# Turning Q, K, P and the memory rows on four 128x32 column tiles instead of one 128x128 tile

## The chip, the core and the metric

The kernel runs on one core of one Trainium2 chip. The metric is the device time of one execution in microseconds; lower is better. Every time below comes from this kernel's runs or from the one execution that was profiled.

## What is computed

Two attention layers, written side by side into one output of 2048 tokens by 1280 columns, in bfloat16. The change touches only the second one, B, a recurrent memory transformer that goes through the tokens in segments of 32:

```python
mem = mem0                                             # 8 rows of 640
for s in range(n_seg):                                 # 64 segments
    h = concatenate([mem, x[:, 32 * s:32 * s + 32]])   # 40 tokens
    q, k, v = h @ Wq, h @ Wk, h @ Wv                   # 32 heads of 192
    p = softmax(mask(q @ k.T * scale))
    o = (p @ v) @ Wo                                   # 40 x 640
    mem = o[:, :8]                                     # into the next segment
    outs.append(o[:, 8:])
```

The first, A, is a sliding window attention over the same number of tokens. It stands ahead of B and is the same in both kernels.

## The kernel before

**Stages.** `part_a` runs first, for some 180 us. Then `part_b` runs 64 segments one after the other. A segment needs its memory rows from the segment before, so the segments are a chain. The 32 heads are handled in four groups `g` of eight; `segment` writes the order of all PE (TensorE) work by hand, and PE keeps that order. The orders on DVE (VectorE), ACT (ScalarE), POOL and SP are made by the framework's scheduler when the program is built, and are then fixed.

**Projections.** `project32` (L443) makes Q, K or V of 32 tokens for one group: for each of five slices of 128 input features, four matmuls, each with 128x32 stationary columns (the 32 tokens) and 384 moving weight columns, on four column tiles (`tile_position=(0, 32 * j)`), into four strips of 32 partitions of one accumulator `acc` (128x384, three buffers). Where a group is renewed (`RENEW`), the last 8 tokens of the next four segments are projected too, as a second set of 32 ("ahead"). `to_sb` casts an accumulator to `sb` (bf16).

**Turns.** `turn` (L456) transposes `sb`, strip by strip of 128 columns, by three matmuls against the identity, 128x128 stationary and 128 moving columns each, into a PSUM tile `pt`. `spread` copies `pt` into `QT`, `KT` or a waiting block `Lb`. `turn_late` does so for the ahead tokens. All copies out of PSUM go through `evacuate` (L423), which alternates between ACT and DVE.

**Attention.** `scores` (L515) takes `QT` and `KT`, on 128x64 and then on 64x64 tiles, into `Sps`. `softmax` runs on DVE (scale and mask L522, maximum `mx` L526, subtraction L527, sum `sm` L530, reciprocal L531) with the exponential on ACT (L528). `put_p` (L540) writes the weights `P` on DVE, two instructions, one for the 32 main tokens and one for the late ones. `turn_p` (L547) transposes both halves of `P` by two 128x128 transposes into a bf16 PSUM tile, copied to `PT`. `mix` (L564) multiplies `PT` with the values on 32x128 and 32x64 tiles, and `project_out` (L578) accumulates the output `Y` over the groups on 128x64 tiles.

**Seam of two segments.** ACT casts `Y` to `row` (L643); meanwhile PE finishes one ahead projection `ql`. `memory_rows` (L589) transposes the 8 memory rows of `row` into `pt` by six matmuls with 8 moving columns: four of 128x128, and between the second and the third of these two of 128x64. DVE copies the result into the next segment's input `HX` (L592). Then follows `turn_late` of `ql`, and the next segment's first projection, which reads `HX`.

**Weights.** Most weights stay in SBUF; 23 blocks of a segment's weights are streamed by SP through a ring of five slots (`t`), each load being issued when its slot comes free.

The order of a segment on PE around the turns, `tq`, `tk` being turns:

```python
tq[1] = project_qk(s, "q", 1)
tq[0]()
tk[0]()
tk[1] = project_qk(s, "k", 1)
put_p(s, 0, *softmax(scores(0)))
tq[1]()
tk[1]()
tq[2] = project_qk(s, "q", 2)
V[0] = values(s, 0)
soft = softmax(scores(1))
tq[2]()
PT[0] = turn_p()
put_p(s, 1, *soft)
tk[2] = project_qk(s, "k", 2)
mix(0, PT[0], V[0])
```

Of the kernel before, what the change touches and what calls it, by code (L numbers as in the profile page):

```python
# [7 lines left out]
FP32 = mybir.dt.float32  # L8
BF16 = mybir.dt.bfloat16
# [262 lines left out]
def part_b(ctx, tc, B_x, B_mem0, B_Wq, B_Wk, B_Wv, B_Wo, out, ident, n_seg, pre, nbuf, mid):  # L272
    nc = tc.nc
    Dm, H, Dh, M, SEG, L = 640, 32, 192, 8, 32, 40
# [92 lines left out]
    def pool(name, **kw):  # L367
        return ctx.enter_context(tc.tile_pool(name=name, reuse_waits="tile", **kw))
# [12 lines left out]
    ps_x = pool("b_ps_x", bufs=4, space=PSUM)  # L381
# [28 lines left out]
    P = cpool.tile([128, 2, 4, 32], BF16, name="P")  # L410
    OT = cpool.tile([128, 12 * L + PADW], BF16, name="OT")
    free = [cpool.tile([128, 12, M], BF16, name=f"Lb{i}") for i in range(BLOCKS)]
    late = {}
# [7 lines left out]
    def evacuate(dst, src):  # L421
        copies["n"] += 1
        (nc.scalar.copy if copies["n"] % 2 else nc.vector.tensor_copy)(dst, src)  # L423
# [24 lines left out]
    def to_sb(p):  # L448
        sb = qk_sb.tile([128, 384], BF16, tag="sb", name="sb")
        evacuate(sb[:], p[:])  # L450
        return sb

    def turn(sb):
        pt = ps_x.tile([128, 3, 4, 32], FP32, tag="x")
        for c in range(3):
            nc.tensor.matmul(pt[:, c], lhsT=sb[:, 128 * c:128 * c + 128], rhs=ident, start=True, stop=True)  # L456
        return pt

    def spread(dst, src):
# [5 lines left out]
    def turn_late(sb, m, g, s, start):  # L465

        pt = turn(sb)
        T = tokens(QT if m == "q" else KT)
        for t in range(start, next_start(m, g, start)):
            if t == s:  # L470
                dst = T[:, :, 32:L]
            else:
                late[m, g, t] = free.pop(0)
                dst = late[m, g, t][:]
            spread(dst, pt[:, :, :, M * (t % 4):M * (t % 4) + M])

    def project_qk(s, m, g):
        T = QT if m == "q" else KT
        renew = s == 0 or f"{m}{g}" in RENEW[s % 4]
        Xs = [ahead(s), main(s)] if renew else [main(s)]  # L480
        sbs = [to_sb(p) for p in project32(Xs, m, g)]

        def turns():
            if renew:
                turn_late(sbs[0], m, g, s, s)
            else:
                b = late.pop((m, g, s))
                nc.gpsimd.tensor_copy(tokens(T)[:, :, 32:L], b[:])  # L488
                free.append(b)
            pt = turn(sbs[-1])  # L490
            spread(tokens(T)[:, :, 0:32], pt[:])

        return turns
# [48 lines left out]

    def turn_p():

        pt = ps_x.tile([128, 2, 128], BF16, tag="x")
        for late in range(2):
            nc.tensor.transpose(pt[:, late, :], P[:, late].rearrange("p a n -> p (a n)"), ident)  # L547
        PT = one.tile([128, 2, 2, L], BF16, tag="PT")
        evacuate(PT[:], pt[:].rearrange("p l (h n) -> p l h n", h=2)[:, :, :, 0:L])
        return PT  # L550
# [30 lines left out]

    def memory_rows(s, Ysb):
        pt = ps_x.tile([128, 5, M], FP32, tag="x")
        for dc in range(5):
            for gv in range(2):
                c0, c1 = max(128 * dc, 320 * gv), min(128 * dc + 128, 320 * gv + 320)
                if c0 < c1:
                    lo = c0 - 128 * dc
                    nc.tensor.matmul(pt[lo:lo + c1 - c0, dc, :], lhsT=Ysb[:, c0 - 320 * gv:c1 - 320 * gv],  # L589
                                     rhs=ident[:, 64 * gv:64 * gv + M], start=True, stop=True,  # L590
                                     tile_position=(0, lo))
        nc.vector.tensor_copy(HXs[(s + 1) % 2][:, :, 0:M], pt[:])  # L592

    def segment(s):
# [14 lines left out]
# [6 lines that stand above are left out]
        V[1] = values(s, 1)  # L615
        tk[2]()
        PT[1] = turn_p()
        Y = ps_y.tile([128, 320], FP32, tag="y")
        project_out(Y, 0)
# [5 lines left out]
        tq[3]()  # L625
        tk[3]()
        PT[2] = turn_p()
        project_out(Y, 1, range(0, 4))
        put_p(s, 3, *softmax(scores(3)))
# [14 lines left out]
        if not last:  # L644
            project32([ahead(s + 1)], "q", gl, range(3, 5), ql)
            sb = to_sb(ql[0])
            memory_rows(s, Ysb)
            turn_late(sb, "q", gl, s, s + 1)
# [11 lines left out]
def run_all(ctx, tc, A_x, A_wqkv, A_wo, B_x, B_mem0, B_Wq, B_Wk, B_Wv, B_Wo, out, ident):  # L660
    n_seg = B_x.shape[1] // 32

    def mid(emit_loads):
        with ExitStack() as actx:
            part_a(actx, tc, A_x, A_wqkv, A_wo, out, ident, emit_loads)

    part_b(ctx, tc, B_x, B_mem0, B_Wq, B_Wk, B_Wv, B_Wo, out, ident, n_seg=n_seg, pre=110000, nbuf=5,
           mid=mid)
# [59 lines left out]
```

## Time and profile before

| | us |
|---|---|
| median of 3 runs | 2029.89 (2027.99 to 2030.7) |
| the profiled execution | 2024.66 |
| its span, first to last instruction | 2022.8 |
| PE busy | 1945.4 (96% of the span) |
| DVE busy | 1128.3 (56%) |
| ACT busy | 725.6 (36%) |
| mean granted PE clock | 0.994 |

PE's busy time counts an instruction from its start to its modelled end; matmuls overlap, so the time that one matmul takes from PE is read from the distance between starts. PEld is PE's loading of stationary columns, which overlaps its matmuls. L numbers are lines of the kernel before. In a row of the profile "128*32 128x384" means 128 rows by 32 stationary columns, and 128 partitions by 384 moving columns.

### The profile page before, as it was taken

The page shows a single profiled execution, that of the slowest core. Times are in us where ns is not written, and L with a number is a line of the kernel's source. Part 1 is how long each engine was busy: PE and PEld are TensorE (multiplying, and loading weights), DVE is VectorE, ACT ScalarE, POOL GpSimd, SP SyncE. Part 2 cuts the span into 40 slices and gives each one's busy share as a digit, 9 for nine tenths or more (in the row PEclk, how much of TensorE's full clock was granted, in tenths as well). Part 3 has the DMA queues.
Part 4 walks back from the last instruction along what each step waited for, and adds up shares of the span by engine and source line. Part 5 has one row for each costly group of instructions (what it writes and reads, how often), then busy time and mean ns, then how long its engine had stood idle before and what let it go on. Part 6 is the DMA issues. An engine that isn't in the chain of part 4 may idle for free.

```text
span 2022.8 us, 97144 instructions
## 1 busy us (share of the span) xinstructions
PE 1945.4 (96%) x42512; PEld 1243.6 (61%) x42512; DVE 1128.3 (56%) x3622; ACT 725.6 (36%) x2126; POOL 193.6 (10%) x674
## 2 busy tenths in 40 slices
PE   7989999999999999999999999999999999999998
PEld 4656666666666666666666666666666665666665
DVE  5875555555555455555555555555555554555554
ACT  3543333333333333333333333333333333333333
POOL 2000000110001101001001001101001001110110
PEclk9999999999999999999999999999999999999999
DMA  9927999999899999999999989999899988989997
GB/s 343 311 76 269 311 300 305 301 302 307 290 305 304 299 288 312 302 304 303 303 299 297 308 292 311 305 303 299 296 298 303 298 304 284 303 293 300 305 302 257
DMA packets 270123, 596.29 MB, mean 295 GB/s; under 512 B 61065, under 2 KB 72841, under 8 KB 269385
## 3 DMA queue, kind: packets, MB, share of 16 engines
q1 hardware_dynamic: 264770, 585.97, 87.9%
q8 instruction: 333, 5.46, 1.1%
q0 software_dynamic: 4928, 4.11, 0.6%
q14 instruction: 92, 0.75, 0.1%
HBM read 576.85 MB, written 18.87 MB: 295 GB/s over the span
## 4 chain that ended last, share of the span: by engine, by line
PE 71%; DMA 19%; DVE 6%; ACT 1%; issue 1%; SPq 1%; POOL 0%; DVEq 0%; POOLq 0%; ACTq 0%
PE acc L443 33%; PE Y L578 18%; DMA t<-wcopy_k 8%; DMA t<-wcopy_o 6%; PE pt L456 6%; PE Sps L515 4%; PE OTps L564 4%; PE pq L95 2%; PE pt L547 2%; DVE sb L423 2%; DMA out_dram<-row 2%; DMA t<-wcopy_v 1%; PE po L161 1%; DMA wcopy_o<-in_B_Wo_dram 1%; PE py L172 1%
## 5 line engine op out<-in xcount | busy, mean ns | idle before, releaser
L443 PEld LDWEIGHTS <-HX 128*32 128x32 bf16 x19380 | 462.7, 96 | 274.3 <-issue 46.5
L578 PEld LDWEIGHTS <-OT 128*64 128x64 bf16 x6144 | 316.8, 109 | 131.0 <-ACT OT L423 20.0
L578 PE MATMUL Y<-wres_o,OT 128*64 128x320 bf16 x3584 | 344.3, 302 | 2.2
L443 PE MATMUL acc<-wres_q,HX 128*32 128x384 bf16 x6460 | 332.6, 328 | 0.5 <-ACT sb L423 0.2
L443 PE MATMUL acc<-t,HX 128*32 128x384 bf16 x4200 | 309.1, 328 | 12.9 <-DMA t<-wcopy_k 10.1
L578 PE MATMUL Y<-t,OT 128*64 128x320 bf16 x2560 | 277.7, 303 | 10.0 <-DMA t<-wcopy_o 9.2
L423 DVE CAST sb<-acc 128x384 bf16<-128x384 f32 x322 | 178.8, 556 | 186.6 <-PE acc L443 171.3
L443 PE MATMUL acc<-wres_v,HX 128*32 128x384 bf16 x4844 | 276.5, 328 | 0.1
L528 ACT ACTIVATE t<-t 128x160 f32<-128x160 f32 x256 | 86.1, 336 | 439.4 <-DVE t L527 439.4
L443 PE MATMUL acc<-wres_k,HX 128*32 128x384 bf16 x3876 | 224.8, 327 | 0.3 <-issue 0.3
L522 DVE SCALAR_TENSOR_TENSOR t<-Sps,mask 128x160 f32<-128x160 f32 x256 | 82.8, 323 | 214.6 <-PE Sps L515 186.6
L423 ACT CAST sb<-acc 128x384 bf16<-128x384 f32 x324 | 153.6, 474 | 125.1 <-PE acc L443 123.5
L456 PE MATMUL pt<-ident,sb 128*128 128x128 bf16 x1938 | 179.4, 221 | 6.9 <-DVE sb L423 1.7
L423 DVE CAST OT<-OTps 128x120 bf16<-128x120 f32 x512 | 125.5, 271 | 97.4 <-PE OTps L564 96.8
L488 POOL COPY QT<-Lb 128x96 bf16<-128x96 bf16 x252 | 67.4, 267 | 1112.0 <-PE Sps L515 955.2
L456 PEld LDWEIGHTS <-sb 128*128 128x128 bf16 x1938 | 110.2, 97 | 82.3 <-issue 32.3
L515 PEld LDWEIGHTS <-QT 128*64 128x64 bf16 (+1 forms) x4096 | 118.9, 109 | 55.1 <-issue 40.5
L423 ACT CAST OT<-OTps 128x120 bf16<-128x120 f32 x512 | 106.0, 258 | 110.7 <-PE OTps L564 110.4
L515 PE MATMUL Sps<-KT,QT 128*64 128x40 bf16 (+1 forms) x4096 | 137.0, 188 | 2.2 <-DVE KT L423 1.0
L530 DVE TENSOR_REDUCE sm<-t 128x4 f32<-128x160 f32 x256 | 81.8, 320 | 78.7 <-ACT t L528 78.7
L564 PEld LDWEIGHTS <-Vst 32*128 32x128 bf16 (+1 forms) x4096 | 62.2, 97 | 82.3 <-issue 60.5
L564 PE MATMUL OTps<-PT,Vst 32*128 32x40 bf16 (+1 forms) x4096 | 109.7, 192 | 0.0
(75 smaller groups left out, 1916.0 us busy)
## 6 DMA issues: line engine op xcount, KB each, us to landing
t<-wcopy_o SPq DMA_DIRECT2D x640, 320.0 KB, 4.3
t<-wcopy_k SPq DMA_DIRECT2D x512, 384.0 KB, 4.8
t<-wcopy_v SPq DMA_DIRECT2D x320, 384.0 KB, 4.8
wres_q<-in_B_Wq_dram SPq DMA_DIRECT2D x20, 384.0 KB, 7.7
wres_v<-in_B_Wv_dram SPq DMA_DIRECT2D x15, 384.0 KB, 7.8
wres_k<-in_B_Wk_dram SPq DMA_DIRECT2D x12, 384.0 KB, 7.7
wres_o<-in_B_Wo_dram SPq DMA_DIRECT2D x14, 320.0 KB, 6.7
wcopy_o<-in_B_Wo_dram SPq DMA_DIRECT2D x10, 320.0 KB, 8.1
```

What stands on the lines that cost most here:

```text
L95: nc.tensor.matmul(pq[32 * d:32 * d + 32], lhsT=wcol[:, k, t, 4 * c + d, :], rhs=xTs[s][:, k, :], start=(k == 0), stop=(k == 4), tile_posi ...
L423: (nc.scalar.copy if copies["n"] % 2 else nc.vector.tensor_copy)(dst, src)
L443: nc.tensor.matmul(ps[n][32 * j:32 * j + 32, :], lhsT=X[:, dc, :], rhs=w[:, 384 * j:384 * j + 384], start=(dc == 0), stop=(dc == 4), tile_ ...
L456: nc.tensor.matmul(pt[:, c], lhsT=sb[:, 128 * c:128 * c + 128], rhs=ident, start=True, stop=True)
L488: nc.gpsimd.tensor_copy(tokens(T)[:, :, 32:L], b[:])
L515: nc.tensor.matmul(Sps[64 * g2:64 * g2 + 64, a, :], lhsT=QT[lo:hi, L * cc:L * cc + 64], rhs=KTt[lo:hi, cc, :], start=(g2 not in seen), sto ...
L522: nc.vector.scalar_tensor_tensor(out=t1[:], in0=Sps[:], scalar=scale, in1=mask[:].unsqueeze(1).to_broadcast([128, 4, L]), op0=ALU.mult, op ...
L528: nc.scalar.activation(t1[:], t1[:], ACTF.Exp)
L530: nc.vector.tensor_reduce(out=sm[:], in_=t1[:], axis=AX.X, op=ALU.add)
L547: nc.tensor.transpose(pt[:, late, :], P[:, late].rearrange("p a n -> p (a n)"), ident)
L564: nc.tensor.matmul(dst, lhsT=V[32 * a:32 * a + 32, e0:e1], rhs=PT[32 * a:32 * a + 32, late, half, :], start=(wide and late == 0 and half = ...
L578: nc.tensor.matmul(Y[64 * gv:64 * gv + 64, :], lhsT=OT[:, L * c:L * c + 64], rhs=w[:, n:n + 320], start=(i == 0 and r == 0), stop=(i == 23 ...
```

## The change

`turn` and `turn_p` go through a new helper `turn32`, which does one 128x128 turn as four matmuls of 128x32 stationary columns, one on each column tile, each writing a strip of 32 partitions. `turn_p` uses plain matmuls instead of transposes, so its PSUM tile is FP32 instead of BF16. `memory_rows` becomes 20 matmuls of 128x32, five on each column tile. All have the tile shape of the projections. The order of `segment` stays.

```diff
+    def turn32(dst, src):
+        for j in range(4):
+            nc.tensor.matmul(dst[32 * j:32 * j + 32, :], lhsT=src[:, 32 * j:32 * j + 32], rhs=ident, start=True,
+                             stop=True, tile_position=(0, 32 * j))
+
     def turn(sb):
         pt = ps_x.tile([128, 3, 4, 32], FP32, tag="x")
         for c in range(3):
-            nc.tensor.matmul(pt[:, c], lhsT=sb[:, 128 * c:128 * c + 128], rhs=ident, start=True, stop=True)
+            turn32(pt[:, c].rearrange("p j n -> p (j n)"), sb[:, 128 * c:128 * c + 128])
         return pt
...
     def turn_p():
-        pt = ps_x.tile([128, 2, 128], BF16, tag="x")
+        pt = ps_x.tile([128, 2, 128], FP32, tag="x")
         for late in range(2):
-            nc.tensor.transpose(pt[:, late, :], P[:, late].rearrange("p a n -> p (a n)"), ident)
+            turn32(pt[:, late, :], P[:, late].rearrange("p a n -> p (a n)"))
...
     def memory_rows(s, Ysb):
         pt = ps_x.tile([128, 5, M], FP32, tag="x")
-        for dc in range(5):
-            for gv in range(2):
-                c0, c1 = max(128 * dc, 320 * gv), min(128 * dc + 128, 320 * gv + 320)
-                if c0 < c1:
-                    lo = c0 - 128 * dc
-                    nc.tensor.matmul(pt[lo:lo + c1 - c0, dc, :], lhsT=Ysb[:, c0 - 320 * gv:c1 - 320 * gv],
-                                     rhs=ident[:, 64 * gv:64 * gv + M], start=True, stop=True,
-                                     tile_position=(0, lo))
+        for n in range(20):
+            gv, j = n // 10, n % 4
+            nc.tensor.matmul(pt[32 * j:32 * j + 32, n // 4, :], lhsT=Ysb[:, 32 * n - 320 * gv:32 * n - 320 * gv + 32],
+                             rhs=ident[:, 64 * gv:64 * gv + M], start=True, stop=True, tile_position=(0, 32 * j))
```

## The prediction, on record before the changed kernel ran

> **What bounds the kernel now.** I read the page first: its busy times and its chain of waits.
>
> ```profile
> PE 1945.4 (96%) x42512; PEld 1243.6 (61%) x42512; DVE 1128.3 (56%) x3622; ACT 725.6 (36%) x2126; POOL 193.6 (10%) x674
> ...
> PE 71%; DMA 19%; DVE 6%; ACT 1%; issue 1%; SPq 1%; POOL 0%; DVEq 0%; POOLq 0%; ACTq 0%
> ```
>
> PE is busy nearly always and holds 71% of the chain, so what PE is spared or charged mostly reaches the end; the 19% on DMAs and 6% on DVE say where it may not. Between the first and the last memory_rows, 216.7 to 1990.0 us, lie 62 segments of 28.6 us, at full granted clock.
>
> Second, the groups by shape. The turns are only
>
> ```profile
> L456 PE MATMUL pt<-ident,sb 128*128 128x128 bf16 x1938 | 179.4, 221 | 6.9 <-DVE sb L423 1.7 <-ACT sb L423 0.6
> ```
>
> and L547 (512 of the same shape, the P turns) and L589 (378 of 8 columns, the memory rows). Their 221 ns overlap, so their price is not there but in the distance between starts, seen third, in PE's timeline:
>
> ```profile
> 1004.19 0.82 PE L443 MATMUL acc<-wres_v,HX 128*32 128x384 bf16 x16
> 1004.95 0.51 PE L456 MATMUL pt<-ident,sb 128*128 128x128 bf16 x6
> 1005.29 0.28 PE L547 MATMUL pt<-ident,P 128*128 128x128 bf16 x2
> 1005.50 0.46 PE L578 MATMUL Y<-t,OT 128*64 128x320 bf16 x4
> ```
>
> The 16 projection matmuls are four groups of four column tiles, whose starts lie 3 to 4 ns apart; groups follow each other every 163 ns (median). The fourth would be followed at 1004.84, but the turn starts at 1004.95. The six turns follow every 56 ns, and L547, of the same tile shape, starts 56 ns after them: no loss. Two more take until 1005.40, and L578, 128x64, starts at 1005.50. So PE loses some 95 ns where the tile shape changes, and nothing where only the line changes (L578 to L515, both 128x64: 132 ns, L578's own pace).
>
> **The change part by part.** All from start distances after the first segment.
>
> *Entry.* From a projection to a turn: 192 times, median 258 ns, of which 163 are the projection's. Both are 128x32 afterwards: 192 x 95 = 18.2 us saved.
>
> *Return.* L456 to L443: 191 times, 149 ns; L547 to L443: 64 times, 158 ns on average. With 57 (next paragraph) left, 191 x 92 + 64 x 101 = 24.0 us saved. The first distance after a switch is also longer: 66 to 67 for 56 in 192 turns, 173 for 163 in 255 projections, 4.7 us more. Gross 46.9. Scores (L515), the out projection (L578) and the fourth P turn stand at other shapes on both sides and keep their switches.
>
> *The turns themselves.* Every 128x128 matmul becomes four of 128x32, on four column tiles. No row shows such a group at 128 columns. Bounds: below, the 56 ns of now (a group streams the same 128 columns); above, the starts of the 64x64 tiles in the scores' second half, 13 to 19 ns apart one by one, four of them 52 to 76 ns. I take the nearest row, groups of four at 384 (163 ns) and, in part A, at 512 columns (216 ns): 53 per 128 columns, hence 163 - 106 = 57. With 1938 + 512 groups, 1.5 ns more each is +3.7 us. Weight loads hide: a pair of 64-column loads with 40-column matmuls (L515) goes every 28 to 32 ns, as many columns as four 32-column loads. PE gets 16,464 more instructions, a fifth; L564 runs 64 instructions in 0.39 us without a stall, so I cost their supply at nothing.
>
> A rule that speaks against this is the Trainium skill's "TensorE: Matmul & The Clock Gate", Part 1, "Wait — 56ns, not 53.3ns?": starts never come closer than about 25 ns. By it a group costs 100 ns, and the turns 2450 x 44 = 108 us more instead of 3.7. The trace disagrees for column tiles: L443's four starts lie within 11 ns.
>
> *Memory rows.* Six matmuls, three shapes, 303 ns from first to last start; afterwards five groups of one shape, 16 (starts alone) to 32 ns (L515's pair) each. I credit nothing:
>
> ```profile
> 1014.27 0.42 ACT L643 CAST row<-Y 128x320 bf16<-128x320 f32 x1 [2.12 <-PE Y L578]
> 1014.73 0.48 ACT L423 CAST sb<-acc 128x384 bf16<-128x384 f32 x1
> ...
> 1014.75 0.47 PE L589 MATMUL pt<-ident,row 128*128 128x8 bf16 x6
> ...
> 1015.26 0.34 PE L456 MATMUL pt<-ident,sb 128*128 128x128 bf16 x3
> ```
>
> The start hangs on ACT's row cast (1014.69, 50 ns before), the turn behind on the sb cast (1015.21, 50 ns before). Both stay, so the earlier rows only make PE idle sooner. Uncovered, 63 x 0.2 = 12.6 us would be gained.
>
> *FP32 for pt.* PT copies on DVE take 232 ns from bf16 (145 of them); by the f32 casts of 120 and 384 columns (274, 558) 160 columns cost 317. On ACT nothing (292 against 295). mix starts at least 212 ns after PT, which covers 85. Only where DVE then makes the next P late does it count; at most 29 x 85 ns = 2.5 us, at least 0: I take 1.2.
>
> *What swallows part of the gain.* PE waits for weights:
>
> ```profile
> PE acc L443 <- DMA t<-wcopy_k: 10.1, 32, 0.9
> PE Y L578 <- DMA t<-wcopy_o: 9.2, 23, 0.8
> ```
>
> By starts rather than idle time, 106 groups come late for a DMA, 36 us in all. Each such transfer was issued some 4.8 us earlier, when its slot came free; a switch saved in between is lost. Seven switches in 28.6 us are 0.12 us in 4.8: up to 106 x 0.12 = 12.7 us; I take 11, as the delay below relieves some.
>
> *The order on DVE and ACT.* SP's order changes only in the first segment, POOL's not. DVE's changes in 198 of some 3,570 places, ACT's in 62. One counts. In segments 3, 4, 7, 8, 11 and so on (from 0), 31 in all, the first softmax has now:
>
> ```profile
> 1307.13 0.55 DVE L423 CAST sb<-acc 128x384 bf16<-128x384 f32 x1
> ...
> 1307.30 0.34 ACT L528 ACTIVATE t<-t 128x160 f32<-128x160 f32 x1 [0.64 <-DVE t L527]
> 1307.67 0.32 DVE L530 TENSOR_REDUCE sm<-t 128x4 f32<-128x160 f32 x1
> ...
> 1308.23 0.39 DVE L540 TENSOR_TENSOR P<-t,sm 128x128 bf16<-128x128 f32 x2
> ...
> 1308.58 0.33 PE L547 MATMUL pt<-ident,P 128*128 128x128 bf16 x2
> ```
>
> The sb cast fills DVE's wait for ACT's exp. Changed, the sum (sm) stands before it: DVE waits idle for exp till 1307.67, then runs sum, sb, reciprocal, P. Queued behind that wait is sb, whose turn (PE, 1308.33) must then wait till 1308.58; behind it P, 0.5 us later, and L547 waits for P (its second half starts 55 ns after P's end in all 31). 31 x 0.52 = +16.1 us; it could be 0 if exp came early enough. In 15 of the 31 ACT also casts an Lb before an sb, which can hold a k turn up to 0.3 us, but ahead of the same P, so nothing is added. In 16 other segments (1, 5, 9...) the maximum (mx) moves ahead of KT and PT copies and fills idle time: P earlier by 0.2 to 0.3 us, I take -3 (0 to -8). Other P-bound turns (45 of 76) lose about one switch: +4.5.
>
> *Sum.* -46.9 + 3.7 + 1.2 + 11 + 16.1 - 3 + 4.5 = -13.4 us. The profiled execution took 2024.7 (span 2022.8 and 1.9 around it), hence 2011; the median shown is 5.2 higher: 2029.9 - 13.4 = 2016.5.
>
> **The rivals.**
>
> *The gain goes through nearly whole.* If DVE's reordering costs nothing and DMAs keep up: -46.9 + 3.7 + 5 = -38, 1992. For it: PE's 96%. Against: P and DMA waits stand in the trace. 0.15.
>
> *It is swallowed.* Each late DMA eats 0.25 us rather than 0.1 (two switches in its window): +15, giving -4 to +4, 2030. For it: issue to landing is over 6 us for some. 0.10.
>
> *Slower: column tiles start one by one.* Place: the 2450 groups; price: the spacing of starts. At 16 ns (the 64x64 tiles) a group takes 64, +17 us more, 2034; at 28 ns (L515's pairs, were that the price of each start) 112, 2450 x 55 = +135, less the swallowed 30 which then vanish: about +90, 2120. It decides from 13.4 / 2450 = 5.5 ns, that is 62.5 ns per group. For it: the one-by-one 64x64 starts; against: 3 to 4 ns in L443 and in L564's 32x64 tiles. The Trainium skill's "TensorEngine Tiling (Array Packing)", "Gotcha 2", says that column tiling turns off fast weight loads, which would point the same way; no run here prices it for 32 columns. 0.20, a third of it at 64.
>
> *The loss is not the shape's.* If the 95 ns came of a change of operands, entries and returns keep it: -5 + 3.7 + 15, 2044. L456 to L547 and L578 to L515 lose nothing, so 0.03.
>
> **How the numbers follow.** The forecast (-4 to -28 us) has 0.52, full gain 0.15, swallowed 0.10, column spacing 0.20, wrong cause 0.03. 0.2% is 4 us, about what a measurement of this kernel can tell from no change. Faster: 0.52 + 0.15 = 0.67; same: the swallowed 0.10 and 0.01 of the mild spacing, 0.11; slower: the other 0.19 and the wrong cause, 0.22. The likeliest case's own range is 2002 to 2026. The range runs from the full gain, 1990, over the swallowed case to the mild form of the spacing, 2036; left out are its strong form (0.13) and the tail of the others.
>
> **What would show it.** L456 with four times the matmuls, groups 57 ns apart; L443 to L456 at 163 ns and back at 57; L589 to L456 still on the sb cast; waits of L547 on P L540 up by some 15 us, in 31 segments; DMA waits up by about 10. The prediction is wrong if groups take over 62 ns, or if the switch distances stay.

## The result, and the profile after

| | before | after |
|---|---|---|
| median of 4 runs, us | 2028.9 (2025.4 to 2030.7) | 2090.1 (2086.9 to 2092.3) |
| ratio, with its 95% interval | | 1.0302 (1.028 to 1.0324) |
| span of the profiled execution, us | 2022.8 | 2090.5 |

The changed kernel is 3% slower; the forecast was 2016.5 us, faster. The page of the changed kernel, its busy line, its instruction queue and its chain of waits:

```profile
PE 1923.1 (92%) x50744; PEld 1266.5 (61%) x50744; DVE 1136.4 (54%) x3622; ACT 726.6 (35%) x2126; POOL 194.4 (9%) x674
...
q8 instruction: 397, 6.50, 1.2%
...
PE 68%; DMA 15%; DVE 9%; issue 5%; ACT 2%; SPq 1%; POOL 0%; DVEq 0%; ACTq 0%; POOLq 0%
```

PE has less to do than before (1923 us for 1945) in a longer span, and the chain has 5% "issue", time in which PE waited for nothing that the profile names; before it was 1%. The queue q8 brings the instructions: 397 packets, 6.50 MB, where the kernel before had this line:

```profile
q8 instruction: 333, 5.46, 1.1%
```

That is 16 KB a packet, and the counts fit PE's: 42,512 matmuls with as many loads are 85,024 instructions, 255.3 a packet; after, 101,488 are 255.6 a packet. So one packet is 256 instructions of 64 bytes, 128 matmuls with their loads.

The waits of PE after (in total us, times, longest us):

```profile
PE acc L443 <- issue: 34.8, 46, 2.2
PE pt L456 <- issue: 21.8, 26, 1.7
PE pt L456 <- DVE sb L423: 16.6, 55, 0.9
PE pt L456 <- ACT sb L423: 7.6, 34, 0.6
...
PE acc L443 <- DMA t<-wcopy_k: 6.2, 14, 1.2
...
PE Y L584 <- DMA t<-wcopy_o: 4.4, 11, 1.1
PE pt L456 <- DVE P L546: 4.0, 13, 0.4
```

The kernel before had one wait of L443 on "issue", of 0.3 us. The new waits stand on projections, turns, scores and mix alike, so they follow no operation. Counting does show a rule. PE's timeline from one of them to the next:

```profile
2032.02 0.48 PE L521 MATMUL Sps<-KT,QT 128*64 128x40 bf16 x11 [0.46 <-issue]
2032.43 0.52 PE L456 MATMUL pt<-ident,sb 128*32 128x128 bf16 x24
2032.77 0.99 PE L443 MATMUL acc<-wres_q,HX 128*32 128x384 bf16 x20
2033.59 0.82 PE L443 MATMUL acc<-t,HX 128*32 128x384 bf16 x16
2034.24 1.15 PE L443 MATMUL acc<-wres_v,HX 128*32 128x384 bf16 x24
2035.31 0.55 PE L521 MATMUL Sps<-KT,QT 128*64 128x40 bf16 x16
2035.79 0.35 PE L456 MATMUL pt<-ident,sb 128*32 128x128 bf16 x12
2035.97 0.23 PE L456 MATMUL pt<-ident,P 128*32 128x128 bf16 x4
2037.35 0.24 PE L456 MATMUL pt<-ident,P 128*32 128x128 bf16 x4 [1.15 <-issue]
```

11 + 24 + 20 + 16 + 24 + 16 + 12 + 4 = 127 matmuls, one packet's worth, and PE stops in the middle of a turn of P whose operands are all there. An instruction packet ran from 2035.14 to 2036.09; PE goes on 1.26 us after its landing. I call such a stop a standstill: a matmul that starts late, released by nothing in the trace, 0.9 to 2.0 us after an instruction packet has landed. By what they add to the usual distance of starts there are 5 of them in the kernel before, 1.2 us together, and 150 after, 89.8 us. The sum depends on what is taken as usual: PE's waits on "issue" alone add up to 73.3 us, and against the median distance of each pair of operations it is 102 us in 155 places, while late starts without a releaser at other times behind a landing make only 8 us. They lie whole packets apart: 127.7 matmuls per packet (median). Before a standstill PE had used up its block of 256 instructions in less time than the next one took to arrive: in the median standstill the packet started 2.8 us after the block's first matmul, took 0.96 us, and PE resumed 1.4 us after it, 5.25 us in all (4.4 to 6.5 in eight of ten). 128 matmuls took 5.71 us in the kernel before (median) and 4.91 in the changed one.

The Trainium skill's "Runtime: NRT & Kernel Launch", section "Instruction fetch mechanics", describes 16 KiB blocks of 256 instructions, which agrees; it also says that a refill is hidden because instructions are dispatched more slowly than blocks arrive. Here 89.8 us of it are not hidden, and the measurement decides.

Where the 67.7 us between the two spans lie, by the distances between starts of matmuls, the standstills taken out of them:

| from one start to the next | before, us | after, us | difference |
|---|---|---|---|
| standstills | 1.2 | 89.8 | +88.6 |
| turn to projection | 39.9 | 14.9 | -25.0 |
| projection to turn | 51.5 | 30.0 | -21.5 |
| within turns | 143.9 | 156.8 | +12.9 |
| within the memory rows | 19.1 | 7.8 | -11.3 |
| memory rows to turn | 14.4 | 25.7 | +11.2 |
| scores to turn | 15.6 | 24.1 | +8.5 |
| mix, out projection, scores, the rest | | | +4 |

Some 5 us of the +12.9 within turns are no loss: a run of turns now ends on four starts that take 10 ns, and this time no longer stands in the rows "turn to".

With the standstills taken out, some -21 us are left. This is an estimate and no measured time, because other waits shrink or hide behind a standstill. The same subtraction gives some -7 us in the pair of kernels that leave out half of `mix` and some -13 us in the pair with less weight traffic (both below).

### The profile page after: what moved, and what is told of

Read it like the earlier page. It is cut to its first block, busy times and chain, and to the rows that moved or that the text cites. A ratio compares the mean times of both kernels' runs of the same rounds, so it can differ in the third digit from the quotient of the medians.

```text
span 2090.5 us, 113608 instructions
## 1 busy us (share of the span) xinstructions
PE 1923.1 (92%) x50744; PEld 1266.5 (61%) x50744; DVE 1136.4 (54%) x3622; ACT 726.6 (35%) x2126; POOL 194.4 (9%) x674
## 4 chain that ended last, share of the span: by engine, by line
PE 68%; DMA 15%; DVE 9%; issue 5%; ACT 2%; SPq 1%; POOL 0%; DVEq 0%; ACTq 0%; POOLq 0%
PE acc L443 30%; PE Y L584 19%; PE pt L456 7%; DMA t<-wcopy_k 6%; PE OTps L570 4%; PE Sps L521 4%; DMA t<-wcopy_o 4%; PE pq L95 2%; DVE sb L423 2%; DMA out_dram<-row 1%; DMA t<-wcopy_v 1%; DMA wcopy_o<-in_B_Wo_dram 1%; DVE sm L536 1%; DVE QT L423 1%; DVE t L533 1%
## 5 line engine op out<-in xcount | busy, mean ns | idle before, releaser
L443 PEld LDWEIGHTS <-HX 128*32 128x32 bf16 x19380 | 480.9, 97 | 293.7 <-issue 95.9
L443 PE MATMUL acc<-wres_q,HX 128*32 128x384 bf16 x6460 | 337.1, 328 | 10.7 <-issue 9.8
L443 PE MATMUL acc<-t,HX 128*32 128x384 bf16 x4200 | 315.3, 327 | 14.8 <-DMA t<-wcopy_k 6.2
L443 PE MATMUL acc<-wres_v,HX 128*32 128x384 bf16 x4844 | 284.3, 328 | 13.9 <-issue 13.5
L443 PE MATMUL acc<-wres_k,HX 128*32 128x384 bf16 x3876 | 229.5, 327 | 7.8 <-issue 7.8
L456 PE MATMUL pt<-ident,sb 128*32 128x128 bf16 x7752 | 193.1, 221 | 42.4 <-DVE sb L423 16.6
L423 ACT CAST sb<-acc 128x384 bf16<-128x384 f32 x324 | 154.0, 475 | 127.7 <-PE acc L443 126.5
L456 PEld LDWEIGHTS <-sb 128*32 128x32 bf16 x7752 | 135.7, 96 | 88.7 <-DVE sb L423 25.7
L521 PEld LDWEIGHTS <-QT 128*64 128x64 bf16 (+1 forms) x4096 | 120.6, 109 | 60.4 <-issue 46.5
```

The costliest lines, as they stand in the source:

```text
L443: nc.tensor.matmul(ps[n][32 * j:32 * j + 32, :], lhsT=X[:, dc, :], rhs=w[:, 384 * j:384 * j + 384], start=(dc == 0), stop=(dc == 4), tile_ ...
L456: nc.tensor.matmul(dst[32 * j:32 * j + 32, :], lhsT=src[:, 32 * j:32 * j + 32], rhs=ident, start=True, stop=True, tile_position=(0, 32 * j))
L521: nc.tensor.matmul(Sps[64 * g2:64 * g2 + 64, a, :], lhsT=QT[lo:hi, L * cc:L * cc + 64], rhs=KTt[lo:hi, cc, :], start=(g2 not in seen), sto ...
```

## The experiments

The theory: the change saves what its switches cost, and loses more because 16,464 more instructions have to come in over the DMA engines. The rivals: the new shape itself is slow (column tiles, weight loads), or the order of DVE's work is.

The kernel before measured 2027 to 2036 us from one set of runs to another. A ratio here is always to the kernel before in the same set; us that are read from two profiles of different sets are less sure by as much.

**More instructions, no other shape (e8_split).** The kernel before, in which the matmuls of four of the five feature slices of every Q projection, and of two of every K projection, are split in two of 192 columns. Turns and memory rows stay as before; 100,528 instructions.

```diff
-                    nc.tensor.matmul(ps[n][32 * j:32 * j + 32, :], lhsT=X[:, dc, :],
-                                     rhs=w[:, 384 * j:384 * j + 384],
+                cuts = (0, 192, 384) if dc and (m == "q" or m == "k" and dc < 3) else (0, 384)
+                for lo, hi in zip(cuts, cuts[1:]):
+                    for j in range(4):
+                        nc.tensor.matmul(ps[n][32 * j:32 * j + 32, lo:hi], lhsT=X[:, dc, :],
+                                         rhs=w[:, 384 * j + lo:384 * j + hi], ...
```

> The kernel before with the same arithmetic and the same tile shapes; only some projection matmuls (q slices 1 to 4, k slices 1 and 2) are two of 192 columns instead of one of 384. 15,504 PE instructions more (100,528; changed kernel 101,488), nothing else on PE but 3 ns more per pair of groups (6 us). DVE's order differs in 46 places from before (a sum ahead of an sb cast). Theory S: standstills 128 matmuls apart, 1.3 to 1.6 us after an instruction packet has landed, 40 to 110 us in all; 2080 to 2150 us. Theory G: no standstills, 2030 to 2055 us (6 us of group spacing, up to 15 of DVE's order).

Measured: 2092.2 us, ratio 1.0327 (1.0294 to 1.036), the same loss as the change's. Lines of its page and of its waits:

```profile
q8 instruction: 393, 6.44, 1.2%
...
PE 74%; DMA 11%; DVE 9%; issue 3%; ACT 2%; SPq 0%; POOL 0%; ACTq 0%; DVEq 0%; POOLq 0%
```

```profile
PE acc L445 <- issue: 28.0, 39, 2.4
```

There are 90 standstills, 48.4 us, a packet's 127.7 matmuls apart again. About 8 us more go to the halved matmuls themselves (their distances +24.5, those from a projection to what follows -16.4). So turns of 128x32 are not needed for the loss. With nearly as many instructions the standstills come to little more than half of the changed kernel's, so the count alone doesn't set them; what else does isn't shown. The experiment isn't pure: in 46 places DVE's order differs as well.

**Fewer instructions, the change kept (e10_after_thin, e11_before_thin).** In both kernels `mix` leaves out the late half of its sum: 8,192 instructions fewer.

```diff
-            for late, V in enumerate((Vst, LV[g])):
+            for late, V in enumerate((Vst,)):
```

> The changed kernel with 8,192 instructions of PE taken out elsewhere: mix leaves out the late half of its sum (the products with the values of the late tokens), 16 matmuls fewer in each of 256 mixes; all turns stay as changed. 93,296 instructions for 101,488. Instruction supply: between the mixed widths (90,898: 27 us of standstills) and the changed kernel (101,488: 90 us) this count, or this count per time, gives 40 to 57 us of standstills; everything else of the change was worth some -21 us, so the distance to the kernel before with the same cut should be +15 to +40 us instead of +61. Rival (each of the 16,464 added matmul instructions costs its own 4 ns or so, wherever it stands, or the column tiles do): the distance to the cut kernel before stays near +61 us.

> The kernel before with the same cut in mix, 76,832 instructions for 85,024. Both theories: hardly any standstills (under 2 us), and the time falls by what the left out matmuls took, 256 times 0.14 to 0.2 us, to 1975 to 1995 us. It is the zero for the cut changed kernel.

Measured: 2051.5 us for the changed kernel, 2016.1 for the one before (0.9913 of the whole one, 0.9891 to 0.9934; the time fell less than expected). The distance is 35 us instead of 61, inside what supply gave, and the standstills are 42.5 us (63) against one of 0.04 us. The switches pay as in the whole kernel (turn to projection -26.3, projection to turn -20.3). PE's waits in this changed kernel:

```profile
PE Y L584 <- DMA t<-wcopy_o: 22.8, 40, 1.7
...
PE pt L456 <- issue: 14.0, 19, 2.1
PE Sps L521 <- issue: 9.4, 11, 1.9
...
PE acc L443 <- issue: 8.4, 12, 2.0
```

Taking instructions out elsewhere gives back 47 us of standstills with every turn still 128x32; a price of the shape would have stayed. Part of that is lost again to weights: the same wait on wcopy_o is 12.7 us in this kernel before.

**Less traffic beside the instructions (e4_after_light, e5_before_light).** In both kernels the 640 loads of streamed out projection weights are left out; a fixed block is read in their place.

```diff
+        if u[0] == "o":
+            return still[:, 0:unit_cols(u)]
         t = wstream.tile([128, SLOT], BF16, tag="ws")
...
-    pre=110000, nbuf=5,
+    pre=110000, nbuf=4,
```

> The changed kernel with 640 of its 1472 streamed weight loads left out (the out projection reads one fixed block in their place, ring of four slots): 205 of 586 MB less for the DMA engines. To be read against the same cut in the kernel before (next run). Theory S with the refill waiting behind the weight loads on the DMA engines: the standstills fall from 90 us to under 45, and this kernel ends at -25 to +15 us of the kernel before with the same cut. Theory S with a refill time of its own: standstills stay at 80 to 100 us and the distance at +50 to +75. Rival G: distance +50 to +75, no matter what the DMAs do.

> The kernel before with the same 640 loads left out, as the control: the 36 us of late weight groups fall to 10 to 25, so 2005 to 2030 us, by both theories; instruction standstills under 3 us, as before.

Measured: 2053.1 and 2038.2 us (1.0069, 1.0043 to 1.0096, and 1.001, 0.9986 to 1.0035, of the whole kernel before). The executions of both spread by 1.1%, so their distance of 15 us is uncertain by some 7. The DMA engines moved some 188 GB/s for 286 in the changed kernel. With the same 101,488 instructions the standstills fell from 89.8 to 27.4 us, and the distance of the two kernels from 61 to 15 us. The packets come sooner: over all blocks, counted on from the standstills, the next packet starts some 2 us (median) after its block's first matmul in the changed kernel and 1.2 us here, 1.6 and 0.8 in the two kernels before, while 128 matmuls took 4.91 and 4.79 us. So how late a packet comes depends on what else the DMA engines carry. Leaving the loads out brought a wait of its own, which is at least part of why neither gets faster than the kernel before (2005 to 2030 us were expected of the second); in the changed kernel it is

```profile
PE acc L447 <- DMA t<-wcopy_v: 49.2, 54, 3.0
```

and 38.1 us (45 times) in the other, where the whole kernel before had 1.1. While PE waits for weights it uses no instructions, so not all of the fall need be due to sooner packets.

**Padding (e1_pad).** The kernel before, with a second load of the same columns ahead of a projection's matmuls: 15,504 instructions more, none of them a matmul.

```diff
+                    if dc:
+                        nc.tensor.ldweights(X[:, dc, :], tile_position=(0, 32 * j))
```

> The kernel before, with one more load of the same stationary columns ahead of every projection matmul of Part B but the first feature slice's: 15,504 PE instructions more (100,528, against 85,024 before and 101,488 in the changed kernel), no other work, no tile shape changed; by the start distances of before (loads 3 to 4 ns apart, groups 163 ns) they take no PE time. Theory S (PE's instructions come in 16 KB pieces of 256, and PE stands still when it has used up one before the next has landed): PE uses up 256 instructions in 4.7 us on average instead of 5.5, near the 4.4 to 5.7 us that the pieces before a standstill took in the changed kernel, so standstills without a releaser, 128 matmuls apart, 1.3 to 1.6 us after the landing of an instruction packet, on a third to a half of the 390 pieces, 0.3 to 0.7 us each: 2070 to 2150 us. Rival G (the cost is in the 128x32 turns themselves or in what they do to DVE and ACT): no change, 2024 to 2035 us.

Measured: 2187.3 us, 1.0742 (1.072 to 1.0764). Only 21 us of it are standstills (48). They lie 107 matmuls per packet apart instead of 127.7, and 42,512 matmuls of 100,528 instructions make 108 in 256: it is instructions that a block holds, not matmuls. But 63 us went to `mix` (137 of 256 are slower, with stretches whose matmuls start 34 or 60 ns apart instead of 3), 30 us to turns, 19 us to the entry of scores and 18 us to the turn behind the memory rows. Why loads without a matmul do this isn't known, so its time says nothing about supply.

**Turn widths chosen by their neighbours (e3_mixed, e6_only64, e7_only32, e9_lastp).** Each turn gets the width of the work around it, 32 beside projections, 64 beside the out projection, 128 elsewhere; memory rows as before. The widths are, in order, those of the turn at the seam, of `tq[0]` with `tk[0]`, `tq[1]` with `tk[1]`, `tq[2]` with the first turn of P, `tk[2]` with the second, `tq[3]` with `tk[3]` and the third, and the fourth turn of P.

```diff
+W_SEAM, W1, W2, W3, W4, W5, W6 = 32, 32, 128, 128, 64, 64, 64        # e3_mixed
+W_SEAM, W1, W2, W3, W4, W5, W6 = 128, 128, 128, 128, 64, 64, 64      # e6_only64
+W_SEAM, W1, W2, W3, W4, W5, W6 = 32, 32, 128, 128, 128, 128, 128     # e7_only32
+W_SEAM, W1, W2, W3, W4, W5, W6 = 128, 128, 128, 128, 128, 128, 64    # e9_lastp
...
-    def turn32(dst, src):
-        for j in range(4):
-            nc.tensor.matmul(dst[32 * j:32 * j + 32, :], lhsT=src[:, 32 * j:32 * j + 32], rhs=ident, ...
+    def turn_by(w, dst, src):
+        for j in range(0, 128, w):
+            nc.tensor.matmul(dst[j:j + w, :], lhsT=src[:, j:j + w], rhs=ident, ..., tile_position=(0, j))
```

> The same number of tile shape changes on PE is avoided as in the changed kernel (7 per segment), with 5,874 instructions more than before instead of 16,464: turns that stand between projections (the first q and k turns, the turn of the seam) on 128x32 tiles, turns that lead into the out projection (last k turn and P of group 1, all of groups 2's end, the last P) on 128x64 tiles, the others and the memory rows as before. DVE's order is that of before but for one place. Theory S: nearly the whole saving of 40 to 47 us minus 10 to 18 lost to DMAs and P, plus 5 to 20 us of instruction standstills: 2000 to 2025 us, faster than before. Rival G: a share of the changed kernel's loss by the number of split turns, 2035 to 2055 us.

> Of e3_mixed only the turns that lead into the out projection, on 128x64 tiles (last k turn and P of group 1, all turns of the step before P of group 2, the last P): 4 tile shape changes per segment avoided, 2,130 PE instructions more than before. Theory S: 256 switches x 93 ns = 24 us gross, a third of it lost to DMAs and P, and instruction standstills at the rate that e3_mixed showed (27 us for 5,874 more), so about 8 us: -16 to +4 us against before. Theory G (a split turn costs in itself): each split matmul the same as in the changed kernel, +3 to +8 us.

> Of e3_mixed only the turns between projections on 128x32 tiles (first q and k turns, the seam's turn): 3 tile shape changes per segment avoided, 3,744 PE instructions more. Theory S: 191 switches x 93 ns = 18 us gross, a third lost, and about 15 us of standstills: -8 to +12 us. Theory G: +10 to +20 us.

> The kernel before with only the last P turn of a segment (between two stretches of the out projection) on 128x64 tiles: 2 tile shape changes per segment avoided for 256 PE instructions more; P's other turns are plain matmuls into an FP32 tile. Theory S: 12 us gross (e3_mixed took 6.6 us from out to turn and a third of 16.6 from turn to out), a third lost to DMAs, 1 us of standstills: -11 to -2 us, the best use of the idea. Theory G: within 2 us of before.

| | instructions | standstills, us (number) | us | ratio to before |
|---|---|---|---|---|
| before | 85,024 | 1.2 (5) | | |
| e9_lastp | 85,280 | 2.8 (7) | 2024.0 | 0.9991 (0.997 to 1.0012) |
| e6_only64 | 87,154 | 7.0 (20) | 2021.7 | 0.9965 (0.9941 to 0.9988) |
| e7_only32 | 88,768 | 13.7 (23) | 2032.7 | 1.0039 (1.0019 to 1.006) |
| e3_mixed | 90,898 | 26.8 (41) | 2033.8 | 0.9988 (0.9973 to 1.0002) |
| after | 101,488 | 89.8 (150) | 2090.1 | 1.0302 (1.028 to 1.0324) |

In this row of kernels the standstills grow with the count of instructions, faster than in proportion. e6_only64 is ahead of both kernels, of the one before by 0.35%, and its interval just excludes no difference: for 2,130 more instructions it takes out the switches into and out of the out projection (turn to out 30.2 to 12.4 us, out to turn 14.8 to 8.4). In its timeline the out projection follows a turn at the turn's own pace, two pairs of 56 ns, with no 95 ns between:

```profile
1004.08 0.28 PE L457 MATMUL pt<-ident,P 128*64 128x128 bf16 x4
1004.19 0.44 PE L585 MATMUL Y<-t,OT 128*64 128x320 bf16 x4
```

e3_mixed was expected to be faster (2000 to 2025 us) and was not: it saves 38.5 us where shapes change and loses nearly all of it, 25.6 us to standstills, some 8 us inside the projections and 3 us inside the out projection. Its waits for streamed weights rose by only 3.7 us, so what the projections lose isn't explained by them alone. Of e9_lastp's 11.5 us the out projection took 5.3 back (it waited 12.9 us for wcopy_o instead of 9.2) and standstills 1.6; what is left can't be told from no change.

**The memory rows undone (e2_norows).** The changed kernel with the six old matmuls, 1,764 instructions fewer.

```diff
-        for n in range(20):
-            gv, j = n // 10, n % 4
...
+        for dc in range(5):
+            for gv in range(2):
...
```

> The changed kernel with the memory rows as before: six matmuls of 128x128 and 128x64 instead of 20 of 128x32, 99,724 instructions for 101,488. Instruction supply, with the memory rows hidden behind the casts of row and sb: the rows take 0.2 us more per seam but nothing comes later for it, and 1,764 instructions fewer take some 6 us per thousand off the standstills: 2076 to 2086 us, standstills some 80 us. Rival (the change of tile shape at the seam counts): two switches per segment come back, 63 times 0.19 us, 2095 to 2105 us.

Measured: 2091.3 us, 1.0283 (1.0243 to 1.0323), span 2087.5: between the two expectations, and no difference from the changed kernel. The standstills fell by 16.2 us, to 73.6. Of the rows' own time 12.7 us came back and 11.4 went from the wait behind them, so the rows stay hidden. Against the rest of the fall stand 1 to 3 us more at half a dozen other places; what causes them isn't known, so a few standstills fewer need not make a kernel faster.

## Why the prediction was wrong

**The step that failed** is one sentence of the turns' paragraph: that 64 instructions of L564 go in 0.39 us without a stall, and that supply is costed at nothing. 64 instructions are a quarter of a block; a short run out of a full block says nothing about the rate at which blocks come. The page had the count: 333 packets, each 128 matmuls, which PE then used up in 5.71 us. With a fifth more instructions it was 4.91, and the standstills show that a refill often takes longer. The term was 0 and measured +88.6 us.

**Entry and return: right.** Projection to turn went from a median of 258 ns to 153, turn to projection from 149 to 46. The forecast of 163 and 57 is met, because these distances start at the last of a group's four matmuls, 10 ns behind the first. (The forecast set 163, counted from the first, against 258, counted from the last, so an entry cost 105 ns and not 95.) The two rows fell by 46.5 us where the forecast had 42.2, and some 2.6 us of it only moved into "within turns". The first distance behind these switches fell as forecast, from 66 to 56 ns in turns and from 173 to 163 in projections. PE's timeline after, at a place like the one shown of before:

```profile
1012.38 0.50 PE L443 MATMUL acc<-wres_v,HX 128*32 128x384 bf16 x8
1012.70 0.68 PE L456 MATMUL pt<-ident,sb 128*32 128x128 bf16 x36
1013.21 0.28 PE L456 MATMUL pt<-ident,P 128*32 128x128 bf16 x8
1013.42 0.46 PE L584 MATMUL Y<-t,OT 128*64 128x320 bf16 x4
```

Two projection groups of 163 ns lead straight to the turn at 1012.70; the 0.11 us before it are gone. The switch to the out projection (1013.32 to 1013.42) stays, as said.

**The turns: right.** A group of four starts every 56 ns (57 expected), its four starts within 10 ns (medians). That ends the rival of single starts, and with it the floor of 25 ns from the Trainium skill's "TensorE: Matmul & The Clock Gate", Part 1, where column tiles are concerned. The row "within turns" rose by 12.9 us for an expected 3.7; 5 us of that are the bookkeeping told above, what the rest is isn't shown.

**Memory rows: right.** Their 11.3 us reappear whole (11.2) in front of the turn behind them. The seam in PE's timeline:

```profile
1022.90 0.29 PE L592 MATMUL pt<-ident,row 128*32 128x8 bf16 x20
1023.48 0.35 PE L456 MATMUL pt<-ident,sb 128*32 128x128 bf16 x12 [0.29 <-DVE sb L423]
```

**FP32: right.** PT's copy on DVE takes 318 ns (317 expected), on ACT 293.

**DVE's order: right in size, sought in the wrong row.** In the 31 segments, from the first scores to the end of P, it takes 4.12 us instead of 3.66 on average (+0.46; 0.52 expected), and P's turn starts 0.47 us later, in 27 of them 55 ns behind P: 14.6 us for 16.1. No run has the new order alone, and some 9 us of standstills lie in the same stretches, so the size is not shown to be the order's; but being 14.6 us at most, DVE's order is not what made the kernel 61 us slower. The waits on P didn't rise, though. The turn of sb ahead of P's waits for the sb cast that stands behind the sum on DVE: of L456's wait on DVE sb, 16.6 us where it was 1.7, 6.0 us stand behind scores, where there were none. Another 8.4 us, and 6.8 of the 7.6 us on ACT sb, stand behind the memory rows. In the 16 segments 1, 5, 9 and so on P came 0.34 us earlier (0.2 to 0.3 expected). There the distance from the turn ahead to P's turn fell by 2.1 us in all, but the one from scores to turn rose by 1.4 and nearly 8 us of standstills lie in between, so the -3 can neither be confirmed nor refuted.

**DMA waits: wrong sign.** They were to swallow 11 us; on wcopy_k they fell from 10.1 to 6.2 us, on wcopy_o from 9.2 to 4.4. It fits that the weights catch up while PE stands still, which would follow from the failed step: in the pair that leaves out half of `mix`, with half the standstills, the waits on wcopy_o rose, from 12.7 to 22.8 us, and those on wcopy_v from 4.0 to 8.8.

With the standstills taken out the rest is some -21 us, and -7 and -13 in the two pairs of experiments, all within the -4 to -28 of the forecast. So one resource was left out, and the others were in order in sum, if not each for itself. The rival "column tiles start one by one" had the right side for a reason that doesn't hold.

## What to carry to other kernels

Count PE's instructions per time before a matmul is split. The span divided by the instruction queue's packets is 6.1 us in the kernel before, with 5 standstills, and 5.3 us in the changed one, with 150, where 4.4 to 6.5 us passed from a block's first matmul until PE resumed with the next. The first trace could have warned: in it the next packet landed some 2.6 us (median) after a block's first matmul, in one of ten after more than 3.5; with the 1.4 us until PE resumes this makes 4 and 5 us, while 128 matmuls took 4.9 us or less in one of ten. Where the two come as close as here, more instructions cost time, however small their matmuls.

A tile shape that fits the neighbours saves its switches (some 95 to 105 ns each) only if it brings few instructions. Of the variants here one came out ahead, by 0.35%: two matmuls of 128x64 for one of 128x128, at the turns beside the out projection. "issue" in a chain, on several unrelated lines, whole blocks of instructions apart, is the sign of it.

## What the hardware showed that had not been expected

PE's instructions share the DMA engines with the weights, and the queue's share of 1.2% gives no hint of it: each packet takes 0.96 us, but PE resumes only 1.4 us after it has landed, and with a third less weight traffic the same stream stood still for 27.4 us instead of 89.8.

A long standstill has an aftermath. The longest in the profile, 2.23 us, ended at 354.75. A stretch before it and two behind it, by windows (length, busy time of PE, PEld, DVE, ACT and POOL with their instructions, granted clock, DMA share, GB/s):

```profile
347.73:349.20 1.47, 1.47 (x54) 0.88 (x57) 0.75 (x4) 0.89 (x3) 0.00 (x0) 1.00 0.93 296
354.75:356.32 1.57, 1.57 (x20) 0.76 (x24) 0.00 (x0) 0.48 (x1) 0.00 (x0) 0.50 0.11 33
357.60:358.60 1.00, 1.00 (x31) 0.56 (x24) 0.63 (x3) 0.42 (x2) 0.00 (x0) 0.71 0.98 255
```

The clock granted is 0.50 for 3.41 us, from 354.76 on, and projection groups go every 0.32 us instead of 0.163. The 69 matmuls behind the stop take 3.61 us, the same 69 elsewhere 2.12 (median of 81 places): a stop of 2.2 us cost about another 1.5. The Trainium skill's "TensorE: Matmul & The Clock Gate", Part 1, has the half clock follow an idle window of about 3.4 us; here 2.2 us of idle time were enough. Such a stop need not bring it: one of 2.35 us between two starts in the changed kernel with half of `mix` left out, at 778.25, is followed by full clock.
